# A linear-attention and FFN kernel: the remainder of the rational activation as two steps over PSUM and a product, and the plain state update in chunks 1 and 2

## The chip, the cores and the metric

The kernel runs on one core of a Trainium2 chip. Its time is the device time of one execution in microseconds (us); less is better. The engines are called as in the profile: PE is TensorE's matmul, PEld its weight load, DVE is VectorE, ACT is ScalarE, POOL is GpSimd and SP is SyncE, which issues DMAs.

## What is computed

The reference is a linear attention whose state decays by a complex factor at each step, followed by a feed-forward layer (FFN) with a rational activation in place of the usual one:

```python
# attention: batch 4, heads 8, 768 steps, head size 48; a = (a_re, a_im), clipped in magnitude
for t in range(S):
    new_re = ar * S_re - ai * S_im
    new_im = ar * S_im + ai * S_re
    kv = einsum('bhd,bhe->bhde', k[:, :, t], v[:, :, t])
    S_re, S_im = (new_re + kv, new_im)
    y[:, :, t] = einsum('bhd,bhde->bhe', q[:, :, t], S_re)
# FFN on x = y laid out as 3072 tokens x 384
h = x @ w_in                                        # 384 -> 2048
P = a[0] + a[1] * h + a[2] * h**2 + a[3] * h**3
Q = 1.0 + abs(b[0]) * abs(h) + abs(b[1]) * h**2
out = (P / (Q + 1e-06)) @ w_out                     # 2048 -> 384
```

## The kernel before

**Attention.** The 768 steps are cut into 6 chunks of 128, and a pair of a chunk `c` and a batch `bb` is a unit: 24 units. For each unit the functions `norm`, `angle` and `trig` make the decays and their phases (tiles `MM`, `T`, `CO`), and `outer` makes the decayed and turned queries and keys: `QK<-QK,RU` and two products `Q<-QK,CO` and `Q<-QK,T` of 768 columns, which DMAs lay out by heads in `HQ`. Then `attn` does the matrix work on TensorE: it transposes the keys into `kT` (L597), makes the scores (L608), which VectorE masks into `ST` (`ST<-at,cmask`, L611), sums values and state into `at` (L624), and hands the result to the FFN as `xT` (`X`), split in a high and a low part except for the first four units. Last, it brings the state `St` up to date for the next chunk, in one of two ways. For `c < TURNED` (L637), eight matmuls `at<-V,kT` of 48 columns (L642, "plain") give the new sum as it lies in `St`, and VectorE adds it (L645). Otherwise eight matmuls `at<-kT,V` of 96 columns (L653, "turned") give it transposed, two heads above each other; it is copied to `ST` by ScalarE or VectorE (L657), a DMA on SP's queue brings it as `kT` (L658), four transposes `at<-ident,kT` turn it back (L663), and VectorE adds it (L667). `TURNED` is 1.

**FFN.** Two units make 256 tokens of each of two batches, or 512 tokens when two pairs go together; a block is 512 columns of hidden units by tokens in one PSUM buffer `ph`. There are 96 blocks: the first 16 are "whole" (full fp32, from the first four units), 80 are "split", where each operand is a high and a low part and three products are summed. `first` (L704) makes `ph`, and `reduce` (L720) adds `g` times `w_out` into three `po` buffers; the reductions stand two blocks behind (L758). Between them lies the rational function, in rings of three `ph`, three `Af` (`AB`), two `Zf` (`ZB`) and four `g` (`GB`). For a split block (lines L739 to L756):

- ScalarE: `Zf<-ph,co` (a square), `Af<-ph` (the absolute value), `Af<-Af,co` (a square), `Zf<-Af,co` (a root of 1/Q), `Zf<-Zf` (its square, 1/Q).
- VectorE: `ph<-Zf,co,ph` (most of the numerator, in place in PSUM), `g<-ph,co,Zf` (the quotient, rounded to fp32r: the high part, `hi`).
- The remainder, which is P minus Q times `hi`, over Q: VectorE `Af<-Af,co,g`, which is (`Af` + `ks`) times `hi`, all in SBUF; VectorE `Af<-ph,co,Af`, which is (`ph` + `c0`) minus it, with `ph` in PSUM; and `g<-Af,Zf`, the low part `lo`, a plain product on GpSimd (35 blocks) or VectorE (45).

**Order.** All operations are first noted as `Op`s of a `Plan`, with the engines on which they may run. Their order and engine are then read from a packed table, `ORDER` (L229), by `Plan.recorded` (L179); each engine runs its own operations in that order. A helper emits most VectorE operations, so L336 stands for it and L351 for ScalarE's. The weights arrive as 64-bit integer pieces and are put together by `fold` (rows L413 to L434) into `wi` and `wo`, and later split into `wiH`, `wh` and their remainders. `rouse` (L676) puts idle matmuls ahead of the FFN. A second, slower path at the program's end is taken only if `bad` is set by the data, and it isn't here.

Of the kernel before, what the change touches and what calls it, by code (L numbers as in the profile page):

```python
# [226 lines left out]


ORDER = (  # L229
    "c-l=^d4Nyl{(jEvW0~_#h&D5%MM=~YB5|!v_AKFEMRp=vWQ);^r9}2MM$s*bGSnbzT5y#Xbt`6sq?q%LW#&8EdG2$*)BWAwAK&A6&%1n<=kq+DcYsJ##*L_o"  # L230
# [3 lines left out]
    "BEN>;k_pLIbA~C3b@3}FV3tcS1|9Grr<hsH^j^hx{E%I++3jT;)V_XdCZm$0k(V<Rsd$QiSEhDzG}5>VpRhHCvm+Xq<~Ef}l#c?}=SHt3lFc=*5y%sYmd_^;"
    "g)By(CC0M{3f)wE>Lo{fT{+seMo+$P`f$3P%{68;-?Qr&iMQQ~)+Y7O9cV({I<Aq=Z}Uc+=ZpA_gH0>1h}E4Q&dRbRoJ)Etcb~HH8hi2(x^al<WjDFqZFe^@"
    "|CDc>e1DA@YtQ<%lKtFRyv!L%X}RMy`$ZJ<b(XLu;_wTPxY6irduTijUEHhkpp;prw~b5kb4z%&X2O{mY+_fwkI}fuC~iPMT=Kh^A@&?!!OwnGr@(*R%&^5w"
    "(7xA%%rtk7y~0a1SLaT~rJ9Mkw>qOZm>1(3hGz0sq_VzqiFz|5?KK`_9p35Wv6*w!pT_LOPxB0lR0Vk)Q0wi}Yxy(p!U)+pL%W~Ud1w3&P+JxZ<ZWh@&17G!"
    "=OEmG#!h>`E;?!E2Ik3%yG*8S!Vy@^lWvN=&U;LMJDIWAhbA0{lYTaCfmLj~;AhP7&vCd`ZgHQs7x@u;p^)87mKTpJT&gI|bkh7M5rcOXv!3|UZ{cj<FvQh5"
    "e>xV;YaKpa$V5DZPnoGK9`GWS?`T|LNArc=^Y|W5aVCsnv(mlnjnO$1<;P0*v^N7TijpI8X35?JS@XKA9g1{!hkcB5@Cf>;>QC{oN%f{`&+*)X!sNcE@4`?l"
    "XBp?A1|C2qzTwRBm&oEX9M4)<D#j=f&Z@g3Y!mnM{0eS_tSMFnTosQ*h*Kzx#o{J=#x3+_3RAc9dwk7?IL_Zuo$cs4i`}ZWFV1qEn}9s8hB#xp8-p8cPh9n{"  # L240
    "nXR5<e2%u;RM(kwOm`d7j%O98NcjAf-|!ApF!$Q4oXGiDiN~3ZLccRo&>yib`K<i}?Nkr9VKrXhD&CFyc#l`)`AJnwF?(Yx|3rc^(oINcZbo{=ieX3WWLHc|"
    "emG}4M!SvdyG+FZvstx!l?HP)tCAw?@f{A3|0nq<+L~?NBJtlz_pp6|ON5ecm?A7hi)EidQ`5{#!8*<EYNmKiv4n%Qel}XN2_DBjzAc7nt`)ap1wWCsSMU|5"
    "^N`~Hj+l5p7x27E)9FiC%8}yiw}tEH@U7d-rqfk6rt)6rh^lOp)-C3BPSl#wvaCJ&%G2X~-W>9(aThv>gXVHC4k$aX<AU$=CA2_8Q^l+0obktoSKTPTnmSSZ"
    "T6jK)X!i?`oXsh!=s(SJuY~D*8JC5QbN+7S`gh#KJ`5p2?3wM&5d&SsB96scE;1MLd>&RL=WqtLU^b6)g^(4YxjlG?(^6=E14r2nKX3<Y;7M`aUi9{V!-F`%"
    "z2<b@6xMW}mY;P@q8*}0yogC|CEG)}`T~#eYj>cnEIla^SIlyo+E(JEEL?KG^d1)ePcc`FUkNkCH2*-l(EcFS`)lR(AI#vhte@D#dmqab?T>L*aY%L+u$v;^"
    "-KoNsW~!Yi)%uW^VFD~;kaFmAC7)-3*r|Y96w61^NpVi)KFs1aQ_1Tsw2OJo%=~5vt?gsdkx$Ium}(1@NAfYT#&FZlyCf?QF?hyfjUsUan;{<K&{keNh$*}z"
    "{kQ?!6qO3N#1rnrc01eQ`-G<Xi%bo#6Nc$qSIr#6LbrmghFO>|O*R<8{<3hd`8jVZ`=F0_=~icf-xqz8&gJfBWpqaw-=(LVuIJ6pWq%IF^5(>!^X4O$>o~*w"
    ";?>7IUgiP}a+76qh8ZKg_0g)2rB#zumuI*T|B~m`F&62jG_O>VuLwuoLbNJ;Di+`mzq`7L=0eXLUc(a!J5<Ak{(e<zG{y^s@4Bzp3Fsx|K8Om6do*L@`8;(P"
    "#Z2Q?{shoTEcGhVs%8(dk-I;i{u9Vjl&l+>e??W&ihHF&6P1f1sncFIbWZwB#D}l4VPYHa827Q2v~Zu>+GdNxmaqk4oe$j!-eR_say+0cOv3VnTss>5#X{NY"
    "Bu-+t-$LwGLr95~Z%3JfI__StuJgEi!fSwZ+=ZXSjZvzOKe@wH^B$5%ajLrQ$ptyRc^qYaDl+i|kDIc*U6`u;UE^k{ZL#vQNtxa&Ue4z)!re5KNEPa-lPZxW"  # L250
    "#o;COI+^O5dNbtKv>AAgyG%E41-{{Yj*$i|<waF!eeq4ca1lg1TFgCDS&70+Ou}YqeMhuV23DJ)((3&t*ZWaCP*D|H0cqx<S5I9-foAp;`vf}-KwYi8$|9b}"
    "YK;%%HX+~zZZ-qFJn>Bh;c2*@)zCqFcb(M`%>4(ph$*wALzSeBL1#E$Ih)LWibSTq)>H2_hqLu<rkUzx;21aRtOLr*I}EzB&pC>(qJ?Sfm2smx*mg1>$)g_P"
    "hE9t3r~I6|6q_sZdWQIJvff{kPph1&?Bs5@-5BI4U98m{)70}l%$>-^W&du)<2a9~hL<_b73Id#;<mz7HDvQ)R1uFEaf*Y68rdV}yi;|vNlc!_6h*j>x!vwo"
    "zf_|2sZ#3Z(&D!G%slQD2xlQ$?g`KBh<WZqPCIX#=Kd<Rsi=M9q#E}siyhQA@4_wao%TJwe=a`%iQl=;ssj)!@ji2(rBD!ue`<DpVedB~J6Z9J*Z#+o8s)yB"
    "2qsD)wwdl;Wh|6x6uEJBt@_kv;>knIMJ%7f26Hv<S@A(kxMR<d|4s3Rym?g25v}^sID$@nviicNIOzMTk0Yjq7t%?~l&A5EYozm>n_-s-mo1cufR7rBxxV&e"
    "oN;_v@tzOI4EHMNODX4xzkkI${tJ5U)UGE?J?|wcKuG*OMz|#=ajB}JqdJjHbQg2QqNX&t4fmMO^V0RdP}u7%%?PQoS4giq%a#e!uNPFS(mHOH7Nv`^A`#TV"
    "DtXdNn$m$EiThtv47Qr1-U{(mjPi59wDBTj*?44V?nX1vv+i^*uq7I4Z8}S_-x7|4n1&d94e322jPg<FsvAKOS7NB}^a0KZ=^?T4S^Uf0;Qdp(^^pFJ6oOZ~"
    "#s+zLE37E}@Q&W|^*uw~%4St(Kf6cv&rmg{h4V+@BVPSnHiOgJ;R9w!d$WX?_xYrvHcc7%RM>k&c4VMj0miFp=i#7YaEO!iEhBs*nX9+`Le5Ss@~Iq;GaK2>"
    "elG_4h{1T2s(qhkMPf1z^I*WoIKrOJSw9}toc{j$#A;qm)K{JSzyq9%`!)MG>zitJE4yP2pT#aA{1rXx;55haSJm>0h#yP8!+lb*kZ^QPXSCu8v2vk5LA7>_"
    "Rh>fr8aoSJ2hF9t?!wS6dEG^O)H4n2LE-%m-O+Xm^XFMxcdHoZPPewsOBF93L?a$ihKq#3*2+y$P%Un%bSz5Q_=%0gVAI^Wb|V|8K8iHDg>}tCHWJpo!5&iw"  # L260
    "UIAOx$8F+3p<<)zag*wzKz#BUe^4Cz;5_aT{|r)x@`(D3@%T--D^`A&ON$bC6%%w{Dt4o7nLk23T_${gnAjjq`>j@d>+nZqZzR9O3BNXui&2WXj7^*e#M_^k"
    "2fS#-J6baqaHNT~OEFF-XQ|&<X2yArSigdPhvnZw-D87ZJU~N<Sm!f8&Upg0-DS4GpRUMFQ9W<LO^VX}s)N~RZ%V!U6^ohZhzB*lg;e=@COFe|tL`ey#mMh`"
    "sl&VKj-J;I<!LEEeRbs%Fx`!{tJPb^YDSS*e6@5UI5k%D<5huq9IMgc>ZO;5>uwO<R7G@E&wi)L_EriLxx&~AAvHmkPIPrYu<uK+b|Qyk<XunPFW<<mQjg)<"
    "vA+~&vgfHseUr0|YX@k|QBO5ZbziF5NRd|V5Ig><U5niyMu)|36Sz+HT`$}1v{E+`Crejjl>Azzo*;{hRe?(s%Y~}>k-}w`{0%a`4#T_-;yPgn?e*-e$nWB7"
    "X1BMK<#)WtwLT=BxLv!yCJx@IerT7v;H7SaZHHRAQ$8gGJ*H0dq<^=w#9t$RK1;{BUlsF=8)Zj0i+l&8oW=eq^$IO;b2!dtcvMKbAXR=$_`gN$RYURoO@7!g"
    "=LElVyj|y?SB_ojTMcyvw<}_`rE6`%C@2<UJXVoHI=W5N(fVTLC>RS?e=C)VlcptVX29w}_H39r4zQ)hf;(EFVm82yw~4}cG1p4NOSwoqu~XV;-56U{{oO);"
    "fqLVRPApY-7L6g|??mz4a@?j~JEUmFiM=N)%fs}xPz)W?jscnq!)PdyHSx-R|FE_M*2T((5`Cd?|GT=HLb26rx~EQ7b}B2fA=S1gpMt*&x$-WkhY9K%FKgb*"
    "9A}nzX`G~f$PJKZHh52~PbpHaLh7H3RF4t50X(Pg3w3gDb<t1h^kGu0VOaSW2IIn2ljn}M>%(jQi{<kAGKxkp8iiii%%EecqLa$kc=~k`vpy=!<x87)2$5Zc"
    "iS}aRLNV`040edrEpm_cXr;SV3@Y*h!h5@&#NtkHb5wsAp*r8szscI5t19Jg%`9bWbqsB#>V^DRoK@oPQO&o(UiolIGg4%U6Sl7$AweW7iqmdHVB-bVLV$rl"
# [838 lines left out]
```

## Time and profile before

| what | value |
|---|---|
| runs | 620.08, 620.59, 620.64 us, median 620.59 |
| profiled execution | 620.44 us, of which the span is 618.7 |
| PE busy | 565.5 us, 91% of the span |
| DVE busy | 563.0 us, 91% |
| ACT busy | 525.0 us, 85% |
| POOL busy | 222.6 us, 36% |
| PE clock, mean | 0.995 of 2.4 GHz |

The span is the time in which the trace shows work. Two engines are equally busy over the whole, so the shares alone don't say which one sets the time; that is read stage by stage below. A row of the timeline gives a start and a length in us; a row of a group gives busy time in us and the mean of one in ns.

### The profile page before, as it was taken

What the parts mean: (1) busy time and instruction counts of PE and PEld (TensorE: products, weight loads), DVE (VectorE), ACT (ScalarE), POOL (GpSimd) and SP (SyncE); (2) the same over time, 40 slices, a digit from 0 to 9 for tenths busy, and PEclk for the clock granted to TensorE, in tenths of its full rate; (3) what the DMA queues carried; (4) which work ended last, traced back from release to release, by engine and by line L of the source; (5) the groups of instructions that cost most, each with busy time, mean ns of one, the idle gap of its engine ahead of it and who ended that gap; (6) DMA issues with size and microseconds to landing.
All of it is one profiled execution on the core that took longest, in us unless ns stands there. A gap on an engine that the chain in (4) does not pass through costs nothing.

```text
span 618.7 us, 12094 instructions
## 1 busy us (share of the span) xinstructions
PE 565.5 (91%) x4486; PEld 481.1 (78%) x4486; DVE 563.0 (91%) x956; ACT 525.0 (85%) x877; POOL 222.6 (36%) x209
## 2 busy tenths in 40 slices
...
GB/s 294 298 230 255 206 60 78 109 147 71 138 94 124 117 147 128 86 89 146 38 120 88 55 88 172 44 130 89 73 89 102 68 45 69 1 51 1 1 1 56
DMA packets 41218, 64.96 MB, mean 105 GB/s; under 512 B 4672, under 2 KB 27200, under 8 KB 41152
## 3 DMA queue, kind: packets, MB, share of 16 engines
...
## 4 chain that ended last, share of the span: by engine, by line
PE 56%; DVE 20%; ACT 13%; DMA 5%; issue 4%; POOL 1%; SPq 1%; DVEq 0%; ACTq 0%; POOLq 0%
PE po L720 23%; PE ph L704 21%; DVE Af L336 4%; PE at L608 4%; PE at L624 4%; DVE g L336 3%; ACT Zf L351 3%; DVE ph L336 2%; ACT SQ L351 2%; DVE T L336 2%; ACT Af L351 2%; DVE MM L336 2%; DVE SQ L336 1%; ACT L351 1%; DVE Q L336 1%
## 5 line engine op out<-in xcount | busy, mean ns | idle before, releaser
L720 PE MATMUL po<-g,wh 128*128 128x512 f32 (+1 forms) x576 | 167.6, 361 | 0.2 <-DVE g L336 0.2
L704 PE MATMUL ph<-X,wiH 128*128 128x512 f32 (+1 forms) x576 | 143.8, 364 | 2.4 <-DVE Af L336 2.3
L720 PE MATMUL po<-g,wo 128*128 128x256 f32 (+1 forms) x462 | 141.0, 366 | 0.5 <-DVE g L336 0.5
L720 PEld LDWEIGHTS po<-g,wh 128*128 128x128 f32 x576 | 103.1, 189 | 17.8 <-issue 1.6
L704 PEld LDWEIGHTS ph<-X,wiH 128*128 128x128 f32 x576 | 96.8, 188 | 20.5 <-DVE Af L336 2.1
L336 POOL TENSOR_TENSOR g<-Af,Zf 128x512 fp32r<-128x512 f32 x35 | 46.3, 1324 | 154.4 <-ACT Zf L351 87.1
L720 PEld LDWEIGHTS po<-g,wo 128*128 128x128 f32 x462 | 86.7, 189 | 12.3 <-DVE g L336 0.9
L336 DVE SCALAR_TENSOR_TENSOR ph<-Zf,co,ph 128x512 f32<-128x512 f32 x96 | 71.7, 748 | 12.5 <-ACT Zf L351 10.3
L351 ACT ACTIVATE Zf<-Af,co 128x512 f32<-128x512 f32 x80 | 57.7, 721 | 25.2 <-DVE ph L336 24.4
L336 DVE SCALAR_TENSOR_TENSOR g<-ph,co,Zf 128x512 fp32r<-128x512 f32 x80 | 59.7, 746 | 17.5 <-ACT Zf L351 16.8
L351 ACT ACTIVATE Zf<-ph,co 128x512 f32<-128x512 f32 x96 | 65.3, 680 | 8.6 <-POOL g L336 4.2
L351 ACT ACTIVATE Af<-Af,co 128x512 f32<-128x512 f32 x96 | 69.0, 720 | 1.6
L351 ACT ACTIVATE Af<-ph 128x512 f32<-128x512 f32 x96 | 56.3, 589 | 14.9 <-PE ph L704 14.3
L704 PE MATMUL ph<-X,wi 128*128 128x512 f32 (+1 forms) x264 | 67.3, 358 | 0.0
L336 DVE SCALAR_TENSOR_TENSOR Af<-Af,co,g 128x512 f32<-128x512 f32 x80 | 64.7, 808 | 2.3
L336 DVE SCALAR_TENSOR_TENSOR Af<-ph,co,Af 128x512 f32<-128x512 f32 x80 | 59.6, 745 | 1.2
L704 PEld LDWEIGHTS ph<-X,wi 128*128 128x128 f32 x264 | 45.7, 188 | 8.1
L351 ACT ACTIVATE Zf<-Zf 128x512 f32<-128x512 f32 x80 | 50.4, 630 | 1.9
L608 PE MATMUL at<-HQ 96*128 96x128 f32 x384 | 49.9, 277 | 1.0 <-ACT kT L342 0.9
L608 PEld LDWEIGHTS at<-HQ 96*128 96x128 f32 x384 | 47.6, 191 | 3.6 <-ACT kT L342 1.4
L704 PE MATMUL ph<-wh,wi 128*128 128x256 f32 x192 | 46.6, 393 | 4.1 <-DVE g L336 3.9
L704 PEld LDWEIGHTS ph<-wh,wi 128*128 128x128 f32 x192 | 36.6, 195 | 10.9 <-issue 3.6
...
## 6 DMA issues: line engine op xcount, KB each, us to landing
...
```

What stands on the lines that cost most here:

```text
L336: call = lambda e: getattr(e, kind)(*map(real, args), **{k: real(x) for k, x in kw.items()})
L351: e.activation(o(), i(), f, **kw)
L608: e.matmul(pst[:, i, :], hf[:, 4 * g + i, 1, :], hf[:, 4 * g + i, 0, :], start=True, stop=True)
L624: e.matmul(py[32 * y:32 * y + 32, min(j, 2), :], l, sts[h // 4][:, h % 4, :] if q is None else hf[:, h, 0, :], start=q is None and j == 0, ...
L704: e.matmul(o, wt[f // 4 * NJ + j][:, f % 4 * P:f % 4 * P + P], moving(j, hl), start=n == 0, stop=n == len(prods) - 1)
L720: e.matmul(o[:, cols], wt[:, j * P:j * P + P], gg, start=(f == 0 and n == 0 and cols.start == 0), stop=(f == NFF - 1 and n == len(prods) - ...
```

## The change

For split blocks, the remainder's first step, (`Af` + `ks`) times `g`, is taken apart: a plain product `Af<-Af,g` on GpSimd or VectorE, and a VectorE step `ph<-g,co,ph` that adds -`ks` times `hi` into `ph` in PSUM; for it the constants get one more column (`tmp` = -`ks`). The third step is as before. `TURNED` becomes 3, so that the units of chunks 1 and 2 (8 of them) update their state in the plain way; chunks 3 and 4 stay turned. The table `ORDER` is a new one. Lines move by one to three: L336 is L337, L351 is L352, L642 is L644, L663 is L665, L704 is L706, L720 is L722.

```diff
--- before.py
+++ after.py
@@ -43,7 +43,7 @@
 MM512 = 231.5
 HQB, QB, VB = 2, 2, 2
 WHOLE = 2
-TURNED = 1
+TURNED = 3
 VP = 64
 STAGED = 21
 STAGE_PS = ("ph", "po0", "ph", "po2", "ph")
@@ -227,48 +227,49 @@
 
 
 ORDER = (
-    "c-l=^d4Nyl{(jEvW0~_#h&D5%MM=~YB5|!v_AKFEMRp=vWQ);^r9}2MM$s*bGSnbzT5y#Xbt`6sq?q%LW#&8EdG2$*)BWAwAK&A6&%1n<=kq+DcYsJ##*L_o"
...
-    "8|C^Joa=;dZT}rF*11KBVz65xuK&MCln6JM!{@|?eJp<~Rkv8aPdOHS;i-I|I0P$0;k*Yb=a@)ajygxPqQcKe{0H^W9O3"
+    "c-mc9d7RDV8vp*rY-cd<duHs(3~?)6q*P?z*Fw0mhDsP)!q`G~X>1pb>_Tx3HB+QP6d$E-QBp2uj*J$}yzjy6<M-U}@3{5H{o|N(e#`Sd@AG_@=LM8QMcju7"
...
+    "7msIFoQgtkm4vbrMspC#OvTy4d)*G*iNgOof7t)sxwl3*J0XAO%!#v<-EgeOc}JJCP6)#eeJ(uoZ#n!I98h5R"
 )
 
 
@@ -388,6 +389,7 @@
         e.tensor_tensor(ks, ks, tmp, ALU.subtract)
         e.tensor_tensor(sc, av[:, 3:4], rb, ALU.mult)
         e.tensor_scalar(minus, sc, -1.0, None, ALU.mult)
+        e.tensor_scalar(tmp, ks, -1.0, None, ALU.mult)
 
     plan.op(dict(DVE=(2000, ratios)), ("ab",), ("co",), port=True)
 
@@ -751,7 +753,8 @@
                 g = buf(ff, [P, 2, 512], F32R, "g", GB)
                 hi = lambda g=g: g[:, 0].bitcast(F32)
                 stt(lambda g=g: g[:, 0], tp, c0, tz, (ph, z_, "co"), ((g, 0),))
-                stt(ta, ta, ks, hi, (a_, (g, 0), "co"), (a_,), psum=False)
+                mul(512, ta, ta, hi, (a_, (g, 0)), (a_,), ALU.mult, EN["glo"])
+                vec("scalar_tensor_tensor", 512, tp, hi, tmp, tp, ALU.mult, ALU.add, more=61, r=((g, 0), ph, "co"), w=(ph,), psum=True)
                 vec("scalar_tensor_tensor", 512, ta, tp, c0, ta, ALU.add, ALU.subtract, more=61, r=(a_, ph, "co"), w=(a_,), psum=True)
                 mul(512, lambda g=g: g[:, 1], ta, tz, (a_, z_), ((g, 1),), ALU.mult, EN["glo"])
             pend.append((k, g))
```

By the counts of the two orders, `Af<-Af,g` runs 54 times on POOL and 26 times on DVE, `g<-Af,Zf` 37 and 43 times (35 and 45 before), and of the 16 evacuations `ST<-at` 8 are left, one on DVE (4 before) and seven on ACT (12 before).

The first place is DVE's order at the start, from the masks of the second unit (`ST<-at,cmask`) on; `wi`, `wo`, `po`, `ph`, `wh` and `g` at L413 to L436 are weights being put together. Before:

```order
L336 TENSOR_TENSOR ST<-at,cmask 128x512
L428 SCALAR_TENSOR_TENSOR wi_511<-wi_511,wh_444 128x512
L336 TENSOR_TENSOR ST<-at,cmask 128x512
L432 SCALAR_TENSOR_TENSOR wo_561<-g,po_417 128x384
L428 SCALAR_TENSOR_TENSOR po_533<-po_533,wh_460 128x384
L428 SCALAR_TENSOR_TENSOR ph<-ph,g 128x384
L432 SCALAR_TENSOR_TENSOR wo_590<-g,ph 128x384
L434 SCALAR_TENSOR_TENSOR wo_598<-wh_460,po_533 128x384
L336 TENSOR_TENSOR St<-St,at 96x8x48
```

After:

```order
L337 TENSOR_TENSOR ST<-at,cmask 128x512 x2
L430 SCALAR_TENSOR_TENSOR ph<-ph,wh_420 128x384
L337 TENSOR_TENSOR QK<-QK,RU 128x768
L430 SCALAR_TENSOR_TENSOR wi_538<-wi_538,wh_415 128x512
L337 TENSOR_TENSOR Q<-QK,CO 128x768
L337 TENSOR_TENSOR Q<-QK,T 128x768
L430 SCALAR_TENSOR_TENSOR po_578<-po_578,wh_439 128x384
L425 TENSOR_SCALAR g<-g 128x512
L436 SCALAR_TENSOR_TENSOR wo_609<-wh_420,ph 128x384
L434 SCALAR_TENSOR_TENSOR wo_614<-wh_439,po_578 128x384
```

Behind the masks there now stand `QK<-QK,RU`, `Q<-QK,CO` and `Q<-QK,T` of a later unit.

The second place is PE's order where a unit of an early chunk brings the state up to date (L653 or L644), beside FFN work and values (L624 or L626). Before, in a unit of chunk 1:

```order
L653 MATMUL at<-kT,V 64x96
L653 MATMUL at<-kT,V 48x96
L653 MATMUL at<-kT,V 64x96
L653 MATMUL at<-kT,V 48x96
L653 MATMUL at<-kT,V 64x96
L653 MATMUL at<-kT,V 48x96
L653 MATMUL at<-kT,V 64x96
L653 MATMUL at<-kT,V 48x96
L624 MATMUL at<-ST,V 32x128 x16
```

After:

```order
L706 MATMUL ph<-wh_946,wi_656 128x256
L610 MATMUL at<-HQ_89 128x128 x4
L722 MATMUL po_1225<-g,wo_390 128x256 x2
L722 MATMUL po_1228<-g,wo_390 128x256
L644 MATMUL at<-V,kT 96x48 x8
L626 MATMUL at<-ST,V 32x128 x16
L626 MATMUL at<-HQ_89,St 32x128 x16
L722 MATMUL po_1225<-g,wo_498 128x256 x2
L722 MATMUL po_1228<-g,wo_498 128x256
```

The eight turned matmuls are eight plain ones in one group, and no L665 follows for such a unit.

The third place is DVE's order in the last blocks, where the remainder's steps of one block stand among those of the next. Before:

```order
L336 SCALAR_TENSOR_TENSOR g<-ph,co,Zf 128x512
L336 SCALAR_TENSOR_TENSOR Af<-Af,co,g 128x512
L336 SCALAR_TENSOR_TENSOR ph<-Zf,co,ph 128x512
L336 SCALAR_TENSOR_TENSOR Af<-ph,co,Af 128x512
L336 SCALAR_TENSOR_TENSOR g<-ph,co,Zf 128x512
L336 SCALAR_TENSOR_TENSOR Af<-Af,co,g 128x512
L336 SCALAR_TENSOR_TENSOR Af<-ph,co,Af 128x512
L336 SCALAR_TENSOR_TENSOR ph<-Zf,co,ph 128x512
```

After:

```order
L337 SCALAR_TENSOR_TENSOR Af<-ph,co,Af 128x512
L337 SCALAR_TENSOR_TENSOR g<-ph,co,Zf 128x512
L337 SCALAR_TENSOR_TENSOR ph<-g,co,ph 128x512
L337 SCALAR_TENSOR_TENSOR ph<-Zf,co,ph 128x512
L337 SCALAR_TENSOR_TENSOR Af<-ph,co,Af 128x512
L337 SCALAR_TENSOR_TENSOR g<-ph,co,Zf 128x512
L337 TENSOR_TENSOR Af<-Af,g 128x512
L337 SCALAR_TENSOR_TENSOR ph<-g,co,ph 128x512
```

`Af<-Af,co,g` is gone and `ph<-g,co,ph` stands in its place; the product `Af<-Af,g` is on DVE for the last block and on POOL for the others shown.

## Rows read from the trace of the kernel before

**Rows 1.** The page's head: the span.
```profile
span 618.7 us, 12094 instructions
```

**Rows 2.** Busy time by stretch: length, engines in order PE, PEld, DVE, ACT, POOL, clock.
```profile
0.00:60.62 60.62, 22.23 (x176) 17.23 (x177) 56.05 (x118) 48.95 (x88) 27.10 (x37) 1.00 0.87 269
60.62:74.00 13.38, 10.13 (x43) 8.25 (x43) 12.57 (x23) 12.40 (x22) 4.54 (x4) 0.96 0.79 204
300.00:360.00 60.00, 58.97 (x432) 48.08 (x431) 58.48 (x93) 54.29 (x91) 23.96 (x20) 1.00 0.35 76
480.00:540.00 60.00, 60.00 (x451) 49.51 (x450) 48.66 (x71) 44.25 (x70) 13.96 (x9) 1.00 0.23 47
60.62:613.00 552.38, 543.22 (x4311) 463.87 (x4310) 506.32 (x838) 475.73 (x790) 195.54 (x173) 1.00 0.38 86
```

**Rows 3.** Timeline of TensorE: start, length, engine, line, operation, tiles, records.
```profile
93.27 1.48 PE L642 MATMUL at<-V,kT 128*96 128x48 f32 x16
94.68 1.08 PE L624 MATMUL at<-ST,V 128*32 128x128 f32 x32
...
164.86 0.87 PE L653 MATMUL at<-kT,V 128*64 128x96 f32 x16
165.66 1.56 PE L720 MATMUL po<-g,wo 128*128 128x256 f32 x6
...
203.19 0.43 PE L663 MATMUL at<-ident,kT 112*96 112x112 f32 x4
203.47 0.36 PE L720 MATMUL po<-g,wh 128*128 128x256 f32 x1
```

**Rows 4.** Waits of TensorE: total us, times, longest.
```profile
PE ph L704 <- DVE g L336: 3.9, 2, 3.1
PE ph L704 <- DVE Af L336: 2.3, 4, 0.8
PE at L663 <- DMA kT<-ST: 0.6, 1, 0.6
```

**Rows 5.** Timeline at the first whole block's `g`; in brackets the idle time before.
```profile
71.28 0.75 DVE L336 SCALAR_TENSOR_TENSOR g<-ph,co,Af 128x512 f32<-128x512 f32 x1
72.18 4.51 PE L704 MATMUL ph<-wh,wi 128*128 128x256 f32 x12 [3.05 <-DVE g L336]
```

**Rows 6.** Groups by line and form: busy us, mean ns, idle before.
```profile
L336 DVE SCALAR_TENSOR_TENSOR Af<-Af,co,g 128x512 f32<-128x512 f32 x80 | 64.7, 808 | 2.3
L336 DVE SCALAR_TENSOR_TENSOR Af<-ph,co,Af 128x512 f32<-128x512 f32 x80 | 59.6, 745 | 1.2
L336 POOL TENSOR_TENSOR g<-Af,Zf 128x512 fp32r<-128x512 f32 x35 | 46.3, 1324 | 154.4 <-ACT Zf L351 87.1 <-DVE Af L336 63.5 <-PE po L720 2.2
L336 DVE TENSOR_TENSOR g<-Af,Zf 128x512 fp32r<-128x512 f32 x45 | 32.1, 713 | 0.7
L336 DVE TENSOR_SCALAR ST<-at 112x384 f32<-112x384 f32 x4 | 2.2, 550 | 0.2 <-PE at L653 0.2
L336 DVE TENSOR_TENSOR Q<-QK,CO 128x768 f32<-128x768 f32 x14 | 13.6, 969 | 0.1
```

**Rows 7.** Timeline of VectorE and GpSimd at 455 us.
```profile
454.98 1.87 DVE L336 SCALAR_TENSOR_TENSOR Af<-Af,co,g 128x512 f32<-128x512 f32 x1
455.00 1.29 POOL L336 TENSOR_TENSOR g<-Af,Zf 128x512 fp32r<-128x512 f32 x1
```

**Rows 8.** Timeline of late blocks: TensorE, ScalarE, GpSimd.
```profile
589.44 0.87 PE L704 MATMUL ph<-X,wiH 128*128 128x512 f32 x3
593.63 0.86 PE L704 MATMUL ph<-X,wiH 128*128 128x512 f32 x3
...
591.75 0.69 ACT L351 ACTIVATE Zf<-ph,co 128x512 f32<-128x512 f32 x1
597.93 1.30 POOL L336 TENSOR_TENSOR g<-Af,Zf 128x512 fp32r<-128x512 f32 x1 [1.90 <-DVE Af L336]
...
600.14 0.68 ACT L351 ACTIVATE Zf<-ph,co 128x512 f32<-128x512 f32 x1
```

More of the change, by code (lines that the diff above doesn't have):

```diff
@@ L229 @@
 ORDER = (
-    "c-l=^d4Nyl{(jEvW0~_#h&D5%MM=~YB5|!v_AKFEMRp=vWQ);^r9}2MM$s*bGSnbzT5y#Xbt`6sq?q%LW#&8EdG2$*)BWAwAK&A6&%1n<=kq+DcYsJ##*L_o"
-    "d{)r&V>*b?$Tj_23D+6?98^SzJ}aVtWk_N?PO(0|<qizvAFPXuN%=XeFoac-({l&$j^ryj85qd57|dHR!@TIlC4ZBf%++X%yLeh-XUs0|xuo>m6!d1Andp6m"
-    "dW^$W{*;`;i8jOA5z(^jBAa5TN%1P-Pu`4Grnc?G-}!GA;vr7L+@!;~hF6f1RF-ob?fDrS$iicIG%1u*3Hwo*Em6vk(Us3&MbhP*qo$SnWzIeL-d&Cj-i_GK"
-    "#`u!;a0had2HWLcB9=sqsT^hh;6d}F_m%6|IApr<HXVnUoz&BIvCTOIDTX}iy~V1qNei#cyxhUO<*kpXUb&6UPJS|{AKpyrZ2Q@>9Lh7;%j&3y#w=tMHlUvQ"
@@ L234 @@
[L234 to L269, printed above, removed]
@@ L270 @@
-    "iQK<5FkU&26DC5kt9(U(i8%ZZ5wQrg?SC-{{U08pWhwuvg7W!}Rs{ML3gge!_W*wd%J|JTKwWt(V{}5i&aq(}R1B{u?>T~gp`2&StucRLB<KJ_Ze?4lQPp%9"
-    "8|C^Joa=;dZT}rF*11KBVz65xuK&MCln6JM!{@|?eJp<~Rkv8aPdOHS;i-I|I0P$0;k*Yb=a@)ajygxPqQcKe{0H^W9O3"
+    "c-mc9d7RDV8vp*rY-cd<duHs(3~?)6q*P?z*Fw0mhDsP)!q`G~X>1pb>_Tx3HB+QP6d$E-QBp2uj*J$}yzjy6<M-U}@3{5H{o|N(e#`Sd@AG_@=LM8QMcju7"
+    "RL5nhgj3=mj92dPZw2Iw_i<1j1yT;Bs3-;U9_GkJc^HL~D}Td9sg`&tyE-C~C+jgn>fwrtv$2UcrF>u&l4KoTk^qjV@g@xC^y8)^p=#igT+t0o2Kq^w{?YW4"
+    "d^D93S%}#QKV=u__sjyxVVubrfF|-i9+i1`OKvB;8rUYc<eap|2iPU42{i-1OOYh`#ur#zar)n_fUl)J?<r{tC-G3AWy0}5b2$xH?U3~*Jh3SIN7cd}(#=f*"
@@ new lines @@
+    "@>H3rh;R(ngG@7&NFv(nvF0(vC1z%~U^N!h$-KN<oW!evv$9J*Qr&F@+?FBOE=td~bz~X7QO$7D?2<tkh$}KuBH+jCco0Jpb_ITri>jC1FWY4fR?1yjj5D%1"
+    "LD}B6C(@bCGW&y+sm-Pa_xOgqk0_j|eeH4sJ;e+|bG6V8jEl%i5hF{mSo&kKP7hAGI|`-JgY}$K=a0+t<qTFy4ZX#5!!a4le7{q%5Q(-4I3%S~A9YcWEAN%f"
+    "7$g(W6d%i%l9TXmAVa$8x@c*hhs%DxFR$YQGw+OfG85y}c=o!9Js?}8GSax$O=_~umEky5d)nm}u~UwtO~RnS2U0BBNt1xoMsMV~C(&9yLl(20uKJlX=q1-h"
+    "qjy*bcN#IWTqg6G9o*?|$(Gk}+nu1V%FDJt{w3{Xa-DryH)SW+h(vBJ-xVKPNQSByjKV@$fS?q(2U*|e)Gl*J>N>B=T-<cu!7@B32NO~Q^YEKn$C;{X*+IA+"
@@ new lines @@
+    "yVgzy5)KB!&;xN8thU;j>NOQ{Wij8n;nsJ)cPl&Az2BKGD`8}zbifbtyzFG({v*q=Onn~Q?#3|VJ;ZxZ#`9AJZ>jNin=EsxC8lRxcRxq#gf)SUtX6F_lnf$a"
+    "r3}STbe23;F$~kWaz8mPb?_>(-TgSN2b+!<#Og1R7ZHmL^|P78K5mmy*dspuf;HkpB`3%AqgaNkAN>Qes-qjKun#4Yp74C2Q2c0%Pvk3iuK%>jlW6iX7Ms*)"
+    "8<eFI&z>s`CQrRMn<U98aCfrGi!oE~!z*}QY9U9eV=R_RzHD?ZyB(zsVzsue8fIJQbEZTJ<$mWCcM(##)1buQuC&4selL}(wcp4Z>Mw7eCa=omZE^HXbAaCy"
+    "FokOvY>_p@&}Ot^J?jxiT03xXOX66=XzIxyrV<9rdR@X_4i=iVWKeZ<!e(`g@jP95z>bln_)Wz_+tXOWsL}XV9>H-c$N+M@H&RrheGb1$y2_WSHV&ud0bEn}"
```

31 lines of the change are left out of this document (added).

## The prediction

> **What bounds the kernel now.** I first read the page's head and the table by stretch [rows 1, 2]. The span is 618.7 us; the profiled execution took 620.44, so 1.74 us lie around the span, and the median of the three runs shown, 620.59, is 0.15 above it. The reader is to see two regimes. Up to the first FFN matmul at 60.62 TensorE is busy for 22.23 us and VectorE for 56.05: there VectorE sets the pace. From 60.62 to 613 TensorE is busy for 543.22 of 552.38 us: there it sets the pace, and all of its waits together are 9.2 us. One of them is large: in 60.62 to 74 it has 3.25 us idle, 3.05 of them in one piece ahead of 72.18, and what ends it is the first whole block's `g`, which VectorE began at 71.28 [rows 5]. The table of waits gives the rest [rows 4]: 3.9 us for `g` in two, 2.3 for `Af` in four (a `ph` buffer that comes free late), 0.6 once for the way back of a turned state. The granted clock is 1.00 of 2.4 GHz in the long stretch [rows 2], so a matmul's price doesn't move. Second, VectorE is nearly full in the middle: 58.48 of 60 us in 300 to 360, against 48.66 of 60 in 480 to 540. So here the sum is: what TensorE gets more or less of, plus what is late at the start, plus what the idle 9.2 us give.
>
> **State update of chunks 1 and 2 (8 units).** A turned unit's matmuls begin at 164.86 and the next work at 165.66, so they hold TensorE for 0.80 us; its four transposes go from 203.19 to 203.47, 0.28 us; together 1.08. A plain unit goes from 93.27 to 94.68, 1.41 us [rows 3]. So each of 8 units costs 0.33 more: **+2.6 us** on the engine that sets the end. Both starts are start-to-start, so what overlaps is not counted twice. What it saves lies elsewhere: 8 evacuations of `ST` (3 on VectorE, 0.55 us each [rows 6], 5 on ScalarE), 8 DMAs on SP's queue, and their latency. Of these only one ends a wait of TensorE: 0.6 us at L663, once [rows 4]. I count **-1.0** for relief: this 0.6, and 0.4, half of the longest wait for `Af` (0.8), for a VectorE that meets GpSimd less; its bounds are -0.6 and -1.4.
>
> **The remainder of the 80 split blocks.** Out go 80 `Af<-Af,co,g` of 0.808 us (64.7). In come 80 steps `ph<-g,co,ph`. The trace has none of that form; its nearest row is `Af<-ph,co,Af`, a step of the same operation and size with one operand in PSUM, 0.745, so 59.6 us [rows 6]. Its bounds: the removed operation's 0.808 above (64.7 us), and nothing below 0.713, the plain product's. In come also 80 products `Af<-Af,g`: 26 on VectorE by 0.713 (18.5 us), 54 on GpSimd by 1.324 (71.5 us), taking the row of the `lo` product for either, which is the same operation over the same shapes. Two `lo` products leave VectorE (-1.4) and 3 evacuations (-1.7). VectorE: -64.7 + 59.6 + 18.5 - 1.4 - 1.7 = +10.3 us. GpSimd: +71.5 + 2.6 = +74, of which it has room: 195.54 of 552.38 us are busy [rows 2].
>
> What does this cost TensorE? On its path nothing, by my value, since VectorE has 46 us idle in the long stretch and TensorE waits there 2.3 us for `Af`. What hides it is the stock of FFN work: three `ph` buffers and reductions that stand two blocks behind. From the start of one block's first matmuls to the next is 593.63 - 589.44 = 4.19 us [rows 8]; `ph` comes free 0.7 to 0.8 us later than before, out of three blocks, 12.6 us. Where the cover is gone, VectorE's +10.3 over 80 blocks is 0.13 us in each (rivals).
>
> The removed step also met GpSimd. At 454.98 it took 1.87 us while a GpSimd product of 1.29 began at 455.00 [rows 7], where its neighbour with one operand in PSUM stays at 0.745 on average. 80 x (0.808 - 0.745) = 5.0 us is what such meetings cost VectorE. The Trainium skill, page "SBUF — State Buffer", section "Who interferes with whom", says that a VectorE instruction with two SBUF inputs contends with a GpSimd instruction that reads SBUF, the loser being blocked, and that one with at most one SBUF input doesn't; the trace agrees with 1.87 against 0.745. By the rule the new PSUM step would be free of it; 26 products and 43 `lo` products on VectorE would still meet 91 GpSimd products. In the sum the gain is inside VectorE's 59.6, so it is off TensorE's path either way.
>
> The other side of it is GpSimd: 1.324 against 0.713 for the same product [rows 6]. The Trainium skill, page "GPSIMD Engine Reference", section "4.1 Engine selection", advises VectorE for a two-input elementwise operation, GpSimd being about 2 times slower; the trace agrees with 1.86 times. By that rule the 54 products would lose 54 x 0.611 = 33 us of engine time, which counts only where a block waits for GpSimd.
>
> **The start.** The new order puts other work ahead of the first whole block's `g` on VectorE: the 768-wide `QK` product and two `Q` products, about 0.97 us each [rows 6], 2.9 us. Pricing both orders up to that `g` by the trace's own durations, the whole difference is +3.5. `g` is what ended the 3.05 us wait, VectorE is busy for 12.57 of 13.38 us there, so little absorbs it: upper bound +3.5. On the other side VectorE is idle for 4.57 us before 60.62, and if 4.0 of it lay where the new rows can use it, all of the 3.5 would be taken and 0.5 gained: lower bound -0.5. I take **+2.0**, nearer to the upper since the wait for `g` is the row that decides. The last blocks I count at 0: VectorE makes both products of the last one.
>
> **Sum.** 620.44 + 2.6 + 2.0 - 1.0 = **624.0 us**; with the bounds of the start and the relief, 621.1 to 625.9.
>
> **Rivals.** (1) *Faster.* VectorE loses 5.0 us of meetings, evacuations and DMAs go, and the idle 9.2 us of TensorE shrink. The wait for `g` (3.05) and for `Af` (2.3), 5.9 with L663's 0.6, could go wholly if the start goes the lower bound's way: 620.44 + 2.6 - 5.9 = 617.1. It decides when TensorE's idle falls by more than 2.6 + 1.2. For it: chunk 1's units need no round trip. Against it: more work ahead of the first `g`. By the "SBUF — State Buffer" rule of the Trainium skill this rival has its cause in the meetings. (2) *VectorE becomes the bound in the middle.* 300 to 360 has 1.5 us idle and 11 to 14 blocks, which want 0.13 each, 1.4 to 1.8: full. If 180 to 480 went at VectorE's pace, with some 55 blocks, 55 x 0.13 = +7.2, in place of most of the 2.6, with the start 2.0: 629. Against it: 11.3 idle in 480 to 540. (3) *The `Zf` ring.* It has two buffers. A block's `Zf` is written at 591.75 and last read by GpSimd's `lo` until 599.23, 7.48 us; the next but one is written at 600.14; two blocks of TensorE take 8.38 [rows 8]. With the product on GpSimd the chain hi, product, `Af`, `lo` grows by 1.32 - 0.81 = 0.5 and a hand-over, to 8.0 to 8.2. Beyond 8.38 every such block costs: 0.1 us on 40 of them is +4, so 628. (4) *No change.* The start's extra work is absorbed and relief pays for the plain states: 620.4 + 2.6 - 1.4 - 0.5 = 621.1, or less.
>
> **Chances.** Forecast (621.7 to 626.5) 0.38; faster 0.28; no change 0.17; VectorE's bound 0.09; the ring 0.08. About 0.2%, 1.24 us, is what a measurement of this kernel can tell from no change. Faster 0.28, same 0.17, slower 0.55. Below 616.5 I leave a third of rival 1, above 629.5 half of rivals 2 and 3: range 616.5 to 629.5.
>
> **What would show it.** In 60.62 to 613 TensorE's busy time should rise from 543.2 to about 546, with 12 plain units instead of 4, and no wait at L663 in chunks 1 and 2. The first large wait for `g` should end at 74 to 75.7, not 72.18. `ph<-g,co,ph` should have a mean of 0.745 even beside GpSimd. VectorE in 300 to 360 should stay under 60 busy without TensorE falling below 58.5; if TensorE's share falls there, rival 2 holds; if ScalarE's first `Zf` waits on GpSimd's `g`, rival 3. I am wrong if the wait at the first `g` is no longer than 3.05, or TensorE's idle falls well under 9.

## The result and the profile after

The changed kernel takes 624.92 us (median of 6 runs, 623.44 to 626.81) against 620.22 for the kernel before in the same comparison (619.67 to 620.64): a ratio of 1.008, 95% interval 1.006 to 1.010, so some 5 us slower. The profiled execution has a span of 623.0 and took 624.75.

The page's head, and busy time by stretch as in [rows 2]:

```profile
span 623.0 us, 12106 instructions
```

```profile
0.00:59.38 59.38, 20.65 (x164) 16.14 (x164) 55.65 (x119) 47.54 (x88) 23.57 (x36) 1.00 0.90 287
59.38:74.00 14.62, 13.99 (x79) 12.39 (x79) 14.20 (x27) 14.17 (x25) 4.73 (x7) 1.00 0.78 174
300.00:360.00 60.00, 58.80 (x419) 47.15 (x418) 58.62 (x95) 51.57 (x85) 31.48 (x28) 1.00 0.33 79
480.00:540.00 60.00, 60.00 (x434) 49.48 (x436) 53.37 (x85) 44.59 (x71) 22.51 (x19) 1.00 0.20 47
59.38:616.00 556.62, 547.18 (x4292) 468.17 (x4292) 521.72 (x853) 467.36 (x775) 271.79 (x241) 1.00 0.35 82
```

From the first FFN matmul to the last one TensorE is busy for 547.18 us against 543.22, and idle for 9.4 against 9.0 (9.2 if the stretch before is taken to 613.00, as the forecast did). The first of these matmuls starts at 59.38, 1.24 us earlier. The start has no long wait any more; the timeline of TensorE and VectorE there, which answers to [rows 5]:

```profile
59.38 8.04 PE L706 MATMUL ph<-wh,wi 128*128 128x256 f32 x36 [0.61 <-ACT wh L343]
67.26 1.48 PE L644 MATMUL at<-V,kT 128*96 128x48 f32 x16
68.59 0.72 DVE L337 SCALAR_TENSOR_TENSOR g<-ph,co,Af 128x512 f32<-128x512 f32 x1
69.37 1.56 PE L722 MATMUL po<-g,wo 128*128 128x256 f32 x6 [0.63 <-DVE g L337]
```

The first `g` begins at 68.59 instead of 71.28, and TensorE waits 0.63 us for it instead of 3.05; ahead of that it does the second unit's plain matmuls (1.48), which before lay ahead of the first FFN matmul. Of the 2.7 us by which VectorE is earlier, 1.5 are one row a little ahead of `g`. Before, it ran beside a GpSimd product:

```profile
66.25 2.01 DVE L336 SCALAR_TENSOR_TENSOR SQ<-AA,SQ 128x384 f32<-128x384 f32 x1
66.03 1.82 POOL L336 TENSOR_TENSOR Q<-QK,T 128x768 f32<-128x768 f32 x1
```

In the changed kernel GpSimd is idle at that time:

```profile
63.44 0.53 DVE L337 SCALAR_TENSOR_TENSOR SQ<-AA,SQ 128x384 f32<-128x384 f32 x1
```

The waits of TensorE, as in [rows 4], show what stands there now:

```profile
PE ph L706 <- DVE Af L337: 3.1, 7, 0.9
PE ph L706 <- DVE g L337: 2.0, 2, 1.2
PE at L599 <- DVE St L337: 1.3, 3, 0.6
PE at L610 <- ACT kT L343: 1.0, 2, 0.8
PE at L599 <- DVE X L337: 1.0, 1, 1.0
PE at L665 <- DMA kT<-ST: 0.4, 1, 0.4
```

`DVE St` (1.3) and `DVE X` (1.0) are new at L599; the wait for `kT` (1.0 in two) is not, it was 0.9 in two before. By the source a plain update holds a buffer of the two-deep ring `at` until VectorE has added it to `St`, and the next unit's transposes need such a buffer; but plain updates alone don't make the wait, since it is absent from the old order with plain updates below. The groups that answer to [rows 6]:

```profile
L337 DVE SCALAR_TENSOR_TENSOR ph<-g,co,ph 128x512 f32<-128x512 f32 x80 | 60.0, 750 | 1.0
L337 DVE SCALAR_TENSOR_TENSOR Af<-ph,co,Af 128x512 f32<-128x512 f32 x80 | 59.6, 746 | 3.4 <-POOL Af L337 1.7
L337 POOL TENSOR_TENSOR Af<-Af,g 128x512 f32<-128x512 f32 x54 | 74.9, 1387 | 98.8 <-DVE g L337 87.2 <-ACT ST L343 7.1 <-DVE nok L976 2.5
L337 DVE TENSOR_TENSOR Af<-Af,g 128x512 f32<-128x512 f32 x26 | 18.6, 717 | 0.2
L337 DVE TENSOR_TENSOR Q<-QK,CO 128x768 f32<-128x768 f32 x21 | 24.2, 1153 | 0.7 <-POOL QK L337 0.4 <-ACT CO L552 0.2
```

The new step takes 750 ns, as forecast (745), and the hand-over from GpSimd costs VectorE only 1.7 us of waiting. So by this profile: 1.24 us earlier at the start, 3.96 more work, 0.44 more idle time between the first and the last FFN matmul (9.43 - 8.99, both taken to the end of the last matmul), 3.2 in all; the rest of the span's 4.3 lies behind the last matmul, where this execution takes 7.0 us and the one before took 5.9. That part isn't the change's: over the 14 profiles of this study it goes from 5.8 to 7.1, in kernels with and without the change. Of the 3.96, the state update's own matmuls make 3.2, 26.8 us against 23.6 (the rows before are shown with the second experiment); here L644, L655 and L665:

```profile
59.38:616.00 556.62, 16.52 (x176) 1.00 0.35 82
59.38:616.00 556.62, 6.99 (x128) 1.00 0.35 82
59.38:616.00 556.62, 3.31 (x32) 1.00 0.35 82
```

### The profile page after: what moved, and what is told of

Same layout as the page of the kernel before. It is cut to its first block, busy times and chain, and to the rows that moved or that the text cites. A ratio compares the mean times of both kernels' runs of the same rounds, so it can differ in the third digit from the quotient of the medians.

```text
span 623.0 us, 12106 instructions
## 1 busy us (share of the span) xinstructions
PE 567.8 (91%) x4456; PEld 484.3 (78%) x4456; DVE 578.2 (93%) x972; ACT 515.4 (83%) x863; POOL 295.4 (47%) x277
## 5 line engine op out<-in xcount | busy, mean ns | idle before, releaser
L722 PE MATMUL po<-g,wh 128*128 128x512 f32 (+1 forms) x576 | 167.0, 360 | 0.1
L706 PE MATMUL ph<-X,wiH 128*128 128x512 f32 (+1 forms) x576 | 146.5, 367 | 3.2 <-DVE Af L337 3.1
L722 PE MATMUL po<-g,wo 128*128 128x256 f32 (+1 forms) x462 | 141.4, 367 | 0.6 <-DVE g L337 0.6
L337 POOL TENSOR_TENSOR Af<-Af,g 128x512 f32<-128x512 f32 x54 | 74.9, 1387 | 98.8 <-DVE g L337 87.2
L722 PEld LDWEIGHTS po<-g,wh 128*128 128x128 f32 x576 | 103.1, 189 | 17.6 <-issue 1.0
L706 PEld LDWEIGHTS ph<-X,wiH 128*128 128x128 f32 x576 | 97.1, 189 | 21.6 <-issue 3.2
L722 PEld LDWEIGHTS po<-g,wo 128*128 128x128 f32 x462 | 86.3, 189 | 12.2 <-DVE g L337 0.8
L352 ACT ACTIVATE Zf<-Af,co 128x512 f32<-128x512 f32 x80 | 57.8, 723 | 26.7 <-DVE ph L337 25.2
L337 DVE SCALAR_TENSOR_TENSOR ph<-Zf,co,ph 128x512 f32<-128x512 f32 x96 | 71.9, 749 | 8.3 <-ACT Zf L352 5.5
L352 ACT ACTIVATE Zf<-ph,co 128x512 f32<-128x512 f32 x96 | 65.2, 680 | 17.0 <-POOL g L337 7.2
L337 POOL TENSOR_TENSOR g<-Af,Zf 128x512 fp32r<-128x512 f32 x37 | 50.1, 1354 | 55.1 <-DVE Af L337 31.8
L337 DVE SCALAR_TENSOR_TENSOR g<-ph,co,Zf 128x512 fp32r<-128x512 f32 x80 | 59.6, 745 | 11.7 <-ACT Zf L352 11.0
L352 ACT ACTIVATE Af<-ph 128x512 f32<-128x512 f32 x96 | 56.0, 588 | 17.0 <-PE ph L706 16.8
L352 ACT ACTIVATE Af<-Af,co 128x512 f32<-128x512 f32 x96 | 69.1, 720 | 1.1
L706 PE MATMUL ph<-X,wi 128*128 128x512 f32 (+1 forms) x264 | 67.7, 360 | 0.0
L337 DVE SCALAR_TENSOR_TENSOR Af<-ph,co,Af 128x512 f32<-128x512 f32 x80 | 59.6, 746 | 3.4 <-POOL Af L337 1.7
L337 DVE SCALAR_TENSOR_TENSOR ph<-g,co,ph 128x512 f32<-128x512 f32 x80 | 60.0, 750 | 1.0
L706 PEld LDWEIGHTS ph<-X,wi 128*128 128x128 f32 x264 | 46.0, 189 | 8.2
L352 ACT ACTIVATE Zf<-Zf 128x512 f32<-128x512 f32 x80 | 50.4, 629 | 1.9
L706 PE MATMUL ph<-wh,wi 128*128 128x256 f32 x192 | 44.9, 383 | 2.6 <-DVE g L337 2.0
```

Of the source, the lines that this page charges most:

```text
L337: call = lambda e: getattr(e, kind)(*map(real, args), **{k: real(x) for k, x in kw.items()})
L352: e.activation(o(), i(), f, **kw)
L706: e.matmul(o, wt[f // 4 * NJ + j][:, f % 4 * P:f % 4 * P + P], moving(j, hl), start=n == 0, stop=n == len(prods) - 1)
L722: e.matmul(o[:, cols], wt[:, j * P:j * P + P], gg, start=(f == 0 and n == 0 and cols.start == 0), stop=(f == NFF - 1 and n == len(prods) - ...
```

## The experiments

Comparisons with the kernel before were made on the same chip, each with its own runs of it; these spread over 4 to 6 us (618.5 to 625.3 in all), so that ratios carry intervals of 0.1 to 0.4% to either side. A profile is of one execution, which can lie 1 to 3 us off the median. Four kernels take the change apart. They keep, for each operation that both programs have, the place and the engine of one of the two orders ("old" or "new"); an operation that this order doesn't have goes to the place of the one that it replaces.

### Old remainder in the new order

```diff
-                mul(512, ta, ta, hi, (a_, (g, 0)), (a_,), ALU.mult, EN["glo"])
-                vec("scalar_tensor_tensor", 512, tp, hi, tmp, tp, ALU.mult, ALU.add, ...)
+                stt(ta, ta, ks, hi, (a_, (g, 0), "co"), (a_,), psum=False)
```

> The changed kernel with its own order and its plain updates in chunks 1 and 2, but with the old remainder: the products Af<-Af,g are left out of the order, and Af<-Af,co,g stands where ph<-g,co,ph stood. The output is the reference's. Theory A (the 8 plain units cost TensorE 2.6 us, the remainder is hidden): no change to the changed kernel, 624.2 to 625.6. Rival R (the remainder's extra 10 to 15 us on VectorE and its hand-overs through GpSimd are what costs): back to 620 to 621.5.

It took 633.73 us, a ratio of 1.018 (1.015 to 1.021): 1% slower than the changed kernel, which neither theory had. The group of the step, and TensorE's waits:

```profile
L336 DVE SCALAR_TENSOR_TENSOR Af<-Af,co,g 128x512 f32<-128x512 f32 x80 | 74.6, 933 | 1.6
```

```profile
PE ph L704 <- DVE Af L336: 8.2, 11, 2.0
PE at L597 <- DVE St L336: 2.3, 5, 0.6
```

The old step's mean is 933 ns here against 808 in its own order and 750 for the step over PSUM in this place: 80 x 0.183 = 14.6 us of VectorE, nearly all that leaving out 26 products (18.6) gave back. By the timelines, 21 of its 80 take over 0.95 us here, and 20 of these run while GpSimd runs a `TENSOR_TENSOR`; in the kernel before it is 7, and all 7 do. Of the 80 steps `ph<-g,co,ph` in the changed kernel 69 run beside one, and none takes over 0.76 us. So in the new order the two-SBUF step meets GpSimd's work more often, and the new remainder is worth having there. `ph` comes free late, 8.2 us of waits instead of 3.1.

### Plain updates in the old order

```diff
-TURNED = 1
+TURNED = 3
```

> The kernel before with its own order and remainder, but plain updates in chunks 1 and 2: the plain matmuls stand where the turned ones stood, the addition where the copy to ST stood, copy, DMA and transposes are gone. Theory A: 620.2 + 2.6 = 622.8 (622.2 to 623.4), with TensorE's busy time up by 2.6. Theory R, or a relief that pays for it: 620.0 to 620.8.

It took 621.84 against 621.93, a ratio of 1.000 (0.998 to 1.002), as the second of the two theories had it. The plain updates alone cost nothing that can be measured, at most 0.2% (1.2 us). TensorE's time from its first FFN matmul (at 61.34) on:

```profile
61.34:613.90 552.56, 544.71 (x4279) 1.00 0.38 84
```

TensorE is busy for 1.5 us more than before, and idle for 7.8 instead of 9.0: L663's wait for the DMA is gone from chunks 1 and 2. The matmuls of the state update alone, in the stretch from the first FFN matmul on, by line. Before (L642, L653, L663):

```profile
60.62:613.00 552.38, 2.96 (x32) 1.00 0.38 86
60.62:613.00 552.38, 13.99 (x256) 1.00 0.38 86
60.62:613.00 552.38, 6.68 (x64) 1.00 0.38 86
```

Here (the same lines):

```profile
61.34:613.90 552.56, 15.27 (x160) 1.00 0.38 84
61.34:613.90 552.56, 7.00 (x128) 1.00 0.38 84
61.34:613.90 552.56, 3.31 (x32) 1.00 0.38 84
```

25.6 us against 23.6: the 8 units take 2.0 more, 0.24 each, not the 0.33 of the forecast.

### The new order alone, and the new remainder alone

The first is the new order with this taken back in the changed kernel, beside the remainder as above:

```diff
-TURNED = 3
+TURNED = 1
```

The second is the kernel before, in its own order, with the new remainder:

```diff
-                stt(ta, ta, ks, hi, (a_, (g, 0), "co"), (a_,), psum=False)
+                mul(512, ta, ta, hi, (a_, (g, 0)), (a_,), ALU.mult, EN["glo"])
+                vec("scalar_tensor_tensor", 512, tp, hi, tmp, tp, ALU.mult, ALU.add, ...)
```

> The new order alone: old remainder, turned updates in chunks 1 and 2, put into the new order at the same distances in operations as in the old one. Theory A: what the new order alone is worth, 624.9 - 2.6 = 622.3 or less, since the first whole block's g comes 2.7 us earlier in it; if later waits that belong to the plain update (St at L599, 1.3 us) go too, 621. Theory R: 620 to 621.5, like the old order.

> The new remainder alone, in the old order: ph<-g,co,ph where Af<-Af,co,g stood, the product right ahead of it, on GpSimd or VectorE as in the changed kernel for each block; turned updates. Theory A: 620.2, at most 0.6 more. Theory R: 622.5 to 625.

Both were far worse than any of the theories had it, 643.76 (1.035, 1.032 to 1.038) and 649.64 (1.043, 1.040 to 1.047). In the second, what VectorE and TensorE wait for says why:

```profile
DVE Af L337 <- POOL Af L337: 13.5, 18, 1.9
```

```profile
PE ph L706 <- DVE Af L337: 13.7, 19, 1.4
```

With the product right ahead of its use, VectorE stands still for GpSimd 18 times, and all that is queued behind on VectorE with it. In the changed kernel the same wait is 1.7 us, since its order puts other work between. The first is 10.0 us above the same kernel with plain updates: turned updates were put into an order that wasn't made for their round trip, and L663 waits 3.7 us for the DMA. A good part of the 10 us is the clock, which falls behind waits in three places (TensorE by stretches: length, busy time, granted clock):

```profile
186.00:191.00 5.00, 4.42 (x28) 0.66 0.61 120
206.00:211.00 5.00, 4.78 (x29) 0.66 0.81 108
295.00:303.00 8.00, 7.16 (x26) 0.57 1.01 197
```

That is 1.7 + 1.7 + 3.4 = 6.8 us of full clock; over its runs the mean granted clock is 0.986, with plain updates 0.996. Neither run says what the new order or the remainder would be worth in an order made for it: an order fits one set of durations.

### The new order's start with the old remainder, and the old start with the new one

The first 680 operations (to about the twelfth whole block) are placed by one order, the rest by the other.

> The first 680 operations of the new order (to about the twelfth whole block), then the old order, with the old remainder and the plain updates of chunks 1 and 2; the output is the reference's. In the profiles the changed kernel is 4.8 us ahead at the 13th block and 3.0 behind at the last. Theory S (the new order's start is a gain, the later order with the new remainder a loss): 620.2 + 1.0 (what plain updates cost in the old order by the profile) - 4 to -4.8 = 616.5 to 618. Rival (the lead is only work put off, and is paid back): 620 to 622.

> The changed kernel, output and all, but with the first 680 operations in the old order and on the old engines. If the new order's start is a gain that lasts (4.8 us ahead at the 13th block in the profile): 628 to 629. If what is won at the start is lost again in the middle anyhow: 624 to 626.

The first took 621.21 (1.0002, 0.9986 to 1.0018), as its rival had it; the second 631.06 (1.015, 1.0125 to 1.0175), above either range. Of the second, the timeline of TensorE at the first `g`:

```profile
72.61 2.90 PE L706 MATMUL ph<-wh,wi 128*128 128x256 f32 x6 [2.82 <-DVE g L337]
```

Four kernels with plain updates now stand beside each other: old start and old rest 1.000, new start and old rest 1.000, old start and new rest 1.015, new start and new rest (the changed kernel) 1.008. With the start the same, the new rest costs 0.8% (4.8 us) behind the new start and 1.5% behind the old one. So the loss lies behind operation 680, in the new remainder together with the whole new order of that part; the new start is worth 0.7% (4.4 us) to that rest, and nothing to the old one. Starts and rests that weren't made for each other may lose something at the seam, so these two figures are what the combinations took, not shares of the change.

### Taking work away

Six runs leave work out of one engine, and with it the low part of `g` or most of the states of chunks 1 and 2. For the steps and products the operation keeps its place in the order and emits nothing, as here for the 26 products on VectorE (and likewise for the 54 on GpSimd, for the 80 steps `Af<-Af,co,g`, and for the 80 steps `ph<-g,co,ph`):

```diff
-                mul(512, ta, ta, hi, (a_, (g, 0)), (a_,), ALU.mult, EN["glo"])
+                plan.op(dict(POOL=(pool(512), lambda e, ta=ta, hi=hi: e.tensor_tensor(ta(), ta(), hi(), ALU.mult)),
+                             DVE=(dve(512), lambda e: None)), (a_, (g, 0)), (a_,), port=True)
```

For the states one matmul stands for eight:

```diff
-                for h in range(H):
+                if c:
+                    e.matmul(pd[0:96].rearrange("p h d -> p (h d)"), kT[:, 0], V[:, 0:DM], start=True, stop=True)
+                for h in range(0 if c else H):
                     e.matmul(pd[0:96, h], kT[:, h], V[:, VP * h:VP * h + D], start=True, stop=True)
```

> The changed kernel with one matmul of 384 columns in place of eight of 48 in the plain updates of chunks 1 and 2 (the states of those chunks are wrong); some 0.7 us less of TensorE for each of 8 units. If TensorE's own work goes into the end one to one: -5 to -6 us, 619 to 620. If its waits take it up: less than -2, 623 to 625.

It took 625.17 (1.006, 1.004 to 1.008), from the changed kernel's 1.008. The busy time of TensorE from its first FFN matmul to its last one, and its waits (L708 is L706 there):

```profile
59.77:618.60 558.83, 542.61 (x4180) 1.00 0.36 82
```

```profile
PE ph L708 <- DVE Af L337: 4.9, 8, 1.4
PE at L599 <- DVE St L337: 3.9, 4, 1.8
```

TensorE does 4.6 us less (542.61 for 547.18) and waits 6.8 us more (16.2 for 9.4): the work taken away came back as waits, most of them for VectorE. The profiled execution took 626.40, 1.2 above the median, so some of the 6.8 is its own. These matmuls didn't cost their own time here; the second of the two expectations holds.

> The changed kernel without the 26 products Af<-Af,g on VectorE (left out: in those blocks the low part of g is wrong); 18.6 us less on VectorE. Theory V (TensorE's waits behind the start, 8.8 us against 4.6 in the old order with plain updates, come from a fuller VectorE): 621 to 622.5. Rival H (they come from the hand-over to GpSimd and back): no change within 1 us.

> The changed kernel without the 54 products Af<-Af,g on GpSimd (left out: in those blocks the low part of g is wrong); 74.9 us less on GpSimd and one hand-over less in each. Theory V: 624 to 625, no change within 1 us, apart from VectorE operations that met GpSimd (up to -1). Rival H: 621 to 622.5.

> The changed kernel without its 80 VectorE steps ph<-g,co,ph (left out: the low part of g is wrong), 60.0 us of VectorE's 578. Theory T, with the remainder's VectorE time as what costs: 617 to 619. Theory C: 623 to 626, no gain beyond 2.

Without the products on VectorE 625.07 (1.006, 1.004 to 1.0075), without those on GpSimd 628.51 (1.010, 1.007 to 1.013), without the steps 624.11 (1.004, 1.002 to 1.006). 18.6 us less on VectorE and 74.9 less on GpSimd change nothing that stands clear of the changed kernel's own interval (GpSimd's run is slower than either theory had it), and even 60.0 us less on VectorE give back only half of the loss. The busy times of that last run in the long stretch:

```profile
60.04:616.70 556.66, 546.04 (x4292) 468.40 (x4292) 479.97 (x773) 468.06 (x776) 271.91 (x241) 1.00 0.36 82
```

VectorE is at 86% there, no engine but TensorE is near its limit, and TensorE still waits 10.6 us. But this run takes away more than time: with the step gone nothing stands between GpSimd's product and its use, and VectorE's wait for it grows from 1.7 us to

```profile
DVE Af L337 <- POOL Af L337: 10.1, 19, 1.5
```

So it doesn't show what 60 us of VectorE are worth by themselves. The run without VectorE's products and the one without GpSimd's speak against a full VectorE (theory V) and against the hand-over (theory H), each taken alone; both together were not tried.

> The kernel before without its 80 VectorE steps Af<-Af,co,g (left out: the low part of g is wrong), 64.7 us of VectorE's 563. Theory T (TensorE's own work sets the end, VectorE only adds waits): TensorE's waits behind the start, 5.8 us, mostly go, 615 to 617. Theory C (in the middle the end hangs on chains over ScalarE, VectorE, DMAs and the fixed orders, not on one engine's work): 619 to 622, no gain beyond 2.

> The old order with plain updates in chunks 1 and 2, and again without the 80 steps Af<-Af,co,g (the low part of g is wrong). To be held against the run without the steps and with turned updates: Theory T: with VectorE's load taken away TensorE's 2.6 us come out in full, +2 to +3. Theory C: -1 to +1, as with the steps.

619.53 (0.997, 0.995 to 0.999) and 620.14 (0.998, 0.997 to 0.999). In the old order too, 64.7 us less on VectorE give only 1.9 us, and the plain updates cost 0.6 there, with overlapping intervals: what theory C expected in both. The chains that it names as the cause were not followed. Without the step and with turned updates TensorE's waits stay as they were:

```profile
59.98:610.60 550.62, 541.71 (x4311) 464.20 (x4310) 449.19 (x758) 474.54 (x790) 187.84 (x173) 1.00 0.38 87
```

8.9 us idle, with VectorE at 82%.

## Why the prediction came out as it did

The forecast was 624.0 in a range of 616.5 to 629.5, slower by 3.6; measured were 624.92 and 4.7. Its size is near, but not by the terms of the sum: the two that made the forecast (+2.6 and +2.0) came out at about nothing and below nothing, and the whole loss stands where the sum had 0. The agreement is luck. One of the forecast's own signs of being wrong was met: the wait at the first `g` is shorter than 3.05 us.

- **State update, +2.6 on TensorE.** Less work than that is there. TensorE is busy for 3.96 us more; at the update's own lines (L644, L655, L665) it is 26.8 us against 23.6, of which 1.5 is the second unit's plain update, which moved behind the first FFN matmul, and 1.7 the eight units (2.0 in the old order). The forecast had priced one unit of each kind from start to start. What failed besides is the step from work to time, "on the engine that sets the end". In the old order the plain updates cost 0.000 (-0.002 to +0.002), and 4.6 us taken off the same matmuls in the new one brought the ratio from 1.008 to 1.006, with intervals that overlap, and 6.8 us of new waits. So TensorE is 98% busy and yet its work isn't the bound there: less work ahead of a wait made the waits longer. That each wait ends a chain over ScalarE, VectorE and DMAs fits this, but no run followed such a chain.
- **Relief, -1.0.** TensorE's idle time fell by 1.2 us in the old order with plain updates. In the changed kernel the relief was spent: the waits for `St` (1.3) and `X` (1.0) at L599 took its place.
- **The start, +2.0.** It came out with the other sign. The three products did stand ahead of the first `g`, but VectorE reached it 2.7 us earlier. The sum added up the durations of the rows ahead of `g`; 1.5 us of the difference is the one row `SQ<-AA,SQ` shown above, which before ran beside a GpSimd product. The first FFN matmul also stands 1.2 us earlier. The lower bound (-0.5) didn't reach this. With the old start the new rest took 4.4 us more.
- **The remainder, 0 on TensorE's path.** Its parts were right, 750 ns for the step, 717 for the product on VectorE, 1387 (not 1324) on GpSimd. VectorE's sum was too low: +15.4 us in the long stretch (521.72 against 506.32) instead of 10.3; seven more `Q<-QK,CO` stand on VectorE, with a mean of 1153 ns instead of 969 (24.2 us against 13.6), which the forecast, going by the split blocks and the evacuations, left out. The loss lies behind operation 680 nevertheless: 0.8% between two kernels that differ only there. So this is where the sum had 0 and the runs say about +5, for the new remainder and the new order of that part together.
- **The rivals.** VectorE as the bound (2) is hard to hold after the runs that took work off it: 18.6 us less gave nothing clear. The `Zf` ring (3) did become busier (ScalarE waits 7.2 us in ten for GpSimd's `g`, before 4.2 in five), but it isn't the cause: without VectorE's products that wait was back at 4.3 in nine, and the time was no better (1.006). Without GpSimd's it was 5.5 in nine. The faster rival (1) had its place right: the wait for `g` went, and the step's meetings with GpSimd. The Trainium skill, page "SBUF — State Buffer", section "Who interferes with whom", gives the reason for the latter, and the runs bear it out: 750 ns with one operand in PSUM and 933 with two in SBUF, in the same place, and the long ones beside GpSimd's products.

What stays open is why the new rest is slower. The remainder and its order can't be told apart by these runs, since each remainder is slower still in the other's order (1.018 and 1.043), and no other order made for the new remainder was tried. No version that leaves nothing out beat the kernel before.

The Trainium skill, page "Perfetto Trace Analysis", section "Identifying the Most-Contended Engine", says that the most-contended engine is the one with the highest occupancy, and to optimize it first; for TensorE it does not take the matmuls' busy share as the measure of headroom. In the changed kernel VectorE has the highest occupancy, 93% of the span, and taking 18.6 us off it gave nothing clear; in the kernel before, 64.7 us off its 91% gave 0.3%. The measurement decides.
